# Six first weight loads instead of five, a first up-projection unit in the same steps, and another hand-written order: sliding-window attention with a squared-ReLU MLP on one core

## The chip, the core and the metric

The kernel runs on one core of a Trainium2 chip. The time is that of one execution on the device, in microseconds. TensorE (PE) multiplies, VectorE (DVE) and ScalarE (ACT) do the elementwise work, GpSimd (POOL) issues the loads, which convert float32 to bfloat16 on their way, and SyncE (SP) issues transposes by DMA and the stores. Each engine works through its own instructions in the order in which they are written, and waits for others by semaphores.

## The reference

Eight heads of causal attention with a window of 128 keys and an ALiBi bias, then an MLP without biases whose activation is the square of ReLU:

```python
scores = scale * np.matmul(q, k.transpose(0, 1, 3, 2))        # B=8, H=8, S=576, D=64
mask = (rel >= 0) & (rel < window)                            # window = 128
scores = np.where(mask, scores + bias[None], -1000000000.0)
...
attn = attn / (np.sum(attn, axis=-1, keepdims=True) + 1e-09)
...
x = np.ascontiguousarray(attn_out.transpose(0, 2, 1, 3)).reshape(B * S, H * D)   # 4608 x 512
h = x @ w_in                                                  # w_in 512 x 2048
r = np.maximum(h, 0.0)
g = r * r
return (g @ w_out).astype(np.float32)                         # w_out 2048 x 512
```

## The kernel before

**Tiling.** The 4608 tokens are 40 blocks m: for each of the 8 batches four of 128 tokens and one of 64. The MLP goes over nine groups g of 512 tokens. Attention of later blocks and the MLP of earlier groups run mixed.

**The order.** Every piece of work is a task with a name, planned by `plan.add`; which engine does it, in which buffer or bank, and in which place is written out by hand in the string `ORDER` (lines 60 to 216, some 1,800 items). `Plan.order` (line 272) walks through it and emits the tasks one by one. An item is `name:engine:places`, with a, d, g and s for ACT, DVE, POOL and SP, none for PE. Within an engine the written order is the order of execution. `Plan.order` also estimates start times from constants (`LAND`, `D_ST`, `dma=`, `lat=`); the only thing that these decide in what is emitted is how many filler matmuls `fill` (line 423) puts into an estimated gap of PE in the first microseconds.

**Names.** These are the items that the prediction uses:

- `lk m`, `lq m`, `lkq m`, `lv m`: loads of a block's k, q, both, and v, issued by POOL (lines 608, 614 and 621). `w_in n`, `w_out n`: the loads of the weights (lines 545 and 548). `PIECES` gives the loads of `w_in` in 128-column groups.
- `tp m`, `ev m`: transposes of k and q by PE (line 677) and their copies out, for the first eight blocks; later blocks have `kqT m`, a transpose by DMA that SP issues (line 662). It waits for its `lkq m` and for all the weights, takes one of 7 `kqT` tiles and frees one of 4 `kq` tiles.
- `s m`: scores (line 734); `e m`: exponentials (line 768); `m m`: masks (line 756); `pv m.0`, `pv m.1`: probabilities times values, in two halves of the heads (line 844); `r`, `n`: the reciprocals of the sums and the normalisation (lines 860 and 873).
- `xp m`, or from block 8 on `x m`: the transpose of the attention output into `xT`, by PE (line 893) and by SP's DMA (line 880).
- `u g.r.e`: a step of the up-projection of groups 0 to 2 (line 993); `UNITS` gives the token ranges r and the steps e of each, in 128-column groups. `reluu`, `squ`: its ReLU and its square.
- `us`, `ut`: sums of weights and of x for the products `f g.u.p` (line 1087), the up-projection of groups 3 to 8 by Strassen's scheme, with u from 0 to 3 and products p from 1 to 7. `s1`, `s2`, `s5`: copies of a product out of PSUM into one of eight `f` tiles (lines 444 and 446, on DVE or ACT); `c11`, `c12`, `c22`: sums (line 1108); then ReLU and square.
- `S1` to `S4` (line 1395) and `p g.p.z` (line 1249): the down-projection, by the same scheme, with its own copies into the same eight `f` tiles and sums into them (lines 1330 and 1335), and `st g.p.t`, the stores of the result out of an `f` tile by SP (line 1288). The tile is free again when the store has landed.

**What holds a task up** is the engine's order, its data, the buffer that it takes (the last user must be done), and, for a DMA of POOL, the one eight before it.

Of the kernel before, what the change touches and what calls it, by code (L numbers as in the profile page):

```python
# [15 lines left out]
FIRST = ["k0", "k1", "i0", "v0", "v1", "k2", "v2", "k3", "v3", "i1", "o0", "i2", "i3", "i4", "o1", "o2", "o3", "k4", "k5", "v4", "k6", "k7", "v5", "v6", "v7"]  # L16
# [6 lines left out]
N_PE = 8  # L23
# [5 lines left out]
D_KQ, D_X, D_ST = 2050.0, 1050.0, 750.0  # L29
# [34 lines left out]
ev2.1.0:d ev0.0.0:d one0.2:d tp1.0::7 s2 s0 e0.0:a e2.0:a e2.1:a ev1.0.0:d e0.1:a lv0:g lv2:g lq3:g lv1:g  # L64
w_in1:g w_in0:g w_in2:g lv3:g w_in3:g lk4:g lq4:g b1::0,4 tp1.1::3 pv2.0::7 ev1.1.0:d r2.0:d pv0.0::1 pv0.1::5
s1 n2.0:d r0.1:d r0.0:d n0.0:d tp3.1::3 n0.1:d xp0.0::6 pv2.1::2 x0.0:d r2.1:d ev3.1.0:d mask1.1:a e1.0:a e1.1:a
table:a pv1.0::7 pv1.1::1 b3::5,0 n2.1:d u0.0.1::4 r1.0:d r1.1:d n1.0:d n1.1:d xp2.0::6 s3 u0.0.0::3 xp1.0::2
dist0:d x2.0:a e3.0:a x1.0:a mask1.7:a reluu0.0.0:a:0 u0.2.0::7 mask0.3:a mask1.2:a mask0.1:a mask1.6:a e3.1:a
u0.1.0::1 u0.1.1::6 pv3.0::5 pv3.1::2 u0.2.1::3 u0.0.2::0 squ0.0.0:d one1.2:d reluu0.1.0:a:1 mask0.2:a
reluu0.2.0:a:2 one1.8:d r3.0:d squ0.1.0:d one1.7:d r3.1:d n3.0:d n3.1:d xp3.0::1 x3.0:d one1.5:d reluu0.2.1:a:3  # L70
one1.6:d squ0.2.1:d squ0.2.0:d reluu0.1.1:a:0 mask1.5:a mask1.4:a mask0.7:a mask0.5:a mask1.3:a mask1.0:a
reluu0.0.2:a:1 u0.1.2::7 tp4.0::5 tp4.1::2 ev4.1.0:d squ0.0.2:d u0.2.2::3 ev4.0.0:a reluu0.0.1:a:3 s4.0::6,1
s4.1::0,5 reluu0.1.2:a:2 e4.0:a lk5:g reluu0.2.2:a:1 lk6:g lq5:g lv5:g lq6:g w_in4:g tp5.0::2 u0.0.3::4
u0.3.0::7 tp5.1::6 squ0.0.1:d one1.1:d one1.0:d squ0.1.2:d ev5.0.0:d e4.1:a mask0.0:a mask0.4:a mask0.6:a m4.0:d
ev5.1.0:d squ0.1.1:d lk7:g lv4:g lv6:g lq7:g w_out3:g w_out0:g lv7:g w_out2:g w_out1:g e4.3:a reluu0.3.0:a:3
# [12 lines left out]
zerov10:d s1_0:d:0 kqT10:s ws1.0:d zerokqT11:d kqT11:s squ1.1.1:d p0.2.1 u1.1.5::7 u1.1.0::0 reluu1.1.0:a:3
reluu1.0.5:a:0 reluu1.1.5:a:1 u1.1.7::1 squ1.1.0:d ws1.2:d reluu1.1.7:a:2 u1.1.2::5 u1.1.6::3 squ1.1.7:a
reluu1.1.2:a:3 reluu1.1.6:a:2 u1.1.3::0 lkq12:g lv12:g lkq13:g lkq14:g s8.0::4,7 s8.1::1,5 ws0.2:d c11_0:d  # L90
S4.0.1:d S4.0.0:d squ1.1.5:d e8.0:a e8.1:a e8.2:a e8.3:a p0.5.0::6 u1.1.4::3 s9.0::4,7 s9.1::1,5 p0.5.1 kqT12:s
m8.0:d ws1.1:d m8.1:d reluu1.1.4:a:1 e9.0:a e9.1:a pv8.1::3 pv8.0::4 p0.6.0 p0.6.1 squ1.1.4:d S1.1.0:d
reluu1.1.3:a:1 e9.2:a s5_0:a:1 e9.3:a p0.3.0 lv10:g lv13:g lkq15:g m9.0:d r8.0:d n8.0:d squ1.0.5:d pv9.0::7
zerov11:d m9.1:d r8.1:d us0.1:d S3.0.1:d pv9.1::0 p0.3.1 lv11:g r9.1:d n8.1:d s10.0::1,4 s10.1::5,3 ws1.3:d
squ1.1.6:a s2_0:a:2 c12_0:d us3.1:d r9.0:d n9.0:d n9.1:d ws0.3:d e10.0:a e10.2:a e10.3:a m10.1:d us2.1:d e10.1:a
squ1.1.2:a x8:s p0.7.0 p1.2.0::6 p1.2.1 s12.0::1,5 s12.1::7,3 p0.7.1 lkq16:g e12.0:a e12.3:a squ1.1.3:a e12.2:a
e12.1:a x9:s m10.0:d S2.1.0:d us1.1:d pv10.0::0 pv10.1::4 pv11.0::1 c22_0:d r11.0:d p1.1.0::3 p1.1.1 p0.4.0
r10.0:d S1.1.1:d m12.1:d m12.0:d n11.0:d r10.1:d s1_1:a:3 c11_1:d S2.1.1:d pv11.1::7 pv12.0::5 pv12.1::1 p0.4.1
p1.6.0 r12.1:d n10.0:d r12.0:d n12.0:d S3.1.1:d n10.1:d S3.1.0:d S4.1.1:d r11.1:d n11.1:d u2.0.7::6
reluu2.0.7:a:0 s3_0:a:4 u2.0.6::0 u2.0.3::5 reluu2.0.6:a:2 reluu2.0.3:a:3 squ2.0.3:d n12.1:d us0.3:d squ2.0.6:d  # L100
u2.0.5::4 reluu2.0.5:a:1 kqT13:s kqT14:s kqT15:s kqT16:s lkq17:g lv15:g lkq18:g lv14:g s13.1::6,2 s13.0::7,0
e13.0:a e13.2:a e13.3:a x11:s x12:s p1.5.0::5 p1.5.1 s14.0::1,4 s14.1::7,6 x10:s u2.0.4::2 p1.6.1 S4.1.0:d
e13.1:a m13.0:d m13.1:d s5_1:a:5 e14.0:a e14.1:a s2_1:a:6 e14.3:a squ2.0.5:d p1.3.0 e14.2:a pv13.1::0 pv13.0::1
r13.0:d r13.1:d n13.0:d n13.1:d p1.3.1 m14.1:d s15.0::4,6 s15.1::7,1 u2.0.1::0 p1.7.0 e15.0:a e15.3:a e15.2:a
e15.1:a lkq19:g lv16:g lkq20:g lv17:g c12_1:d us3.3:d us1.3:d squ2.0.7:d st0.7.2:s kqT17:s st0.2.0:s x13:s
kqT18:s st0.7.3:s kqT19:s kqT20:s s16.0::4,5 s16.1::1,7 u2.0.2::6 p1.7.1 us2.3:d m14.0:d e16.0:a e16.1:a
reluu2.0.4:a:3 m16.0:d c22_1:d reluu2.0.1:a:2 squ2.0.1:a e16.3:a e16.2:a u2.1.3::4 u2.1.7::5 reluu2.1.7:a:1
m15.0:d m16.1:d squ2.1.7:d u2.1.1::2 pv14.0::0 pv16.0::7 pv14.1::1 pv16.1::5 reluu2.1.3:a:0 squ2.0.4:d
reluu2.0.2:a:2 squ2.0.2:a reluu2.1.1:a:1 r16.0:d n16.0:d r14.1:d r14.0:d n14.0:d r16.1:d m15.1:d n16.1:d p1.4.0
# [134 lines left out]
class Plan:  # L244
# [5 lines left out]
    FIRST = {"POOL": 1100.0, "SP": 1150.0, "ACT": 1150.0}  # L250
    LAND = {"POOL": 2400.0, "SP": 2200.0, "ACT": 900.0}
# [81 lines left out]
def kernel(  # L333
# [65 lines left out]
    L = N_LEAD  # L399
# [84 lines left out]
    for part in (1, 0):  # L484
        key = EARLY + 2 if part else -1e5 + 1100
# [972 lines left out]
```

## Time and profile before

| | |
|---|---|
| time, median of 3 runs | 294.30 us (293.76 to 294.39) |
| the profiled execution | 293.62 us, of which the span is 291.9 us |
| PE busy | 281.3 us (96%) |
| VectorE busy | 250.7 us (86%) |
| ScalarE busy | 218.9 us (75%) |
| POOL busy | 106.4 us (36%) |
| DMA | 39.64 MB, mean 136 GB/s |

The span runs from the first to the last instruction. Busy time is that of an engine's instructions; an engine that waits is idle. In a row of a timeline the first number is the start in us from the start of the span, the second how long the group lasted, then the engine, the line of the kernel, the operation, the output tile, the input tiles and the count. Brackets at its end give the idle time ahead of it and what ended that. In a row of the waits stand the engine, its line, what it waited for, and the total, the count and the longest wait. Landing times of DMAs are counted from their issue. SPq is SP's instruction queue, in which its transposes and stores are issued; DMA stands for the transfer itself.

### The profile page before, as it was taken

Reading aid. Unit: us, or ns where it says so; the run is one execution under the profiler, and the core shown is the slowest. Engines: PE = TensorE matmul, PEld = TensorE weight load, DVE = VectorE, ACT = ScalarE, POOL = GpSimd, SP = SyncE. Lnnn points to the kernel's source line nnn. Section 1 sums busy time; section 2 is a strip of 40 time slices with the busy share of each in tenths; the row PEclk is TensorE's granted clock in tenths of the full one; section 3 lists DMA queues with packets and bytes.
Section 4 is the critical chain, followed back from the end, with each engine's and each line's share of the span. In section 5 each row is a group of like instructions: output and inputs, shape, how many; then the busy total and the mean of one; then the engine's idle time right before and its main releaser. Section 6 shows DMA issues by size and latency. Waiting matters only on the chain.

```text
span 291.9 us, 8707 instructions
## 1 busy us (share of the span) xinstructions
PE 281.3 (96%) x3480; PEld 243.6 (83%) x3480; DVE 250.7 (86%) x610; ACT 218.9 (75%) x431; POOL 106.4 (36%) x132
## 2 busy tenths in 40 slices
PE   6899999998999999999999999989999999999994
PEld 2688999886888988888888889868898888888884
DVE  2556888897868899999999999979999998999864
ACT  4679976875378786799989998888786846976800
POOL 8968643582663922441737363051000000000000
PEclk9999999999999999999999999999999999999999
DMA  9999999999999999999999999999641222010054
GB/s 125 167 194 172 183 200 155 141 141 159 170 161 175 173 169 168 149 160 177 172 167 142 174 164 140 145 156 150 180 93 57 56 66 63 20 36 2 0 159 151
DMA packets 171497, 39.64 MB, mean 136 GB/s; under 512 B 156992, under 2 KB 171456, under 8 KB 171456
## 3 DMA queue, kind: packets, MB, share of 16 engines
q0 software_dynamic: 115184, 18.10, 92.1%
q1 hardware_dynamic: 55520, 20.39, 41.0%
q10 hardware_dynamic: 752, 0.59, 0.7%
q8 instruction: 27, 0.44, 0.6%
q14 instruction: 14, 0.11, 0.1%
HBM read 36.70 MB, written 9.44 MB: 158 GB/s over the span
## 4 chain that ended last, share of the span: by engine, by line
PE 75%; DMA 11%; POOL 7%; DVE 2%; issue 2%; ACT 1%; SPq 1%; POOLq 0%; DVEq 0%
PE o L1249 31%; PE h L1087 23%; PE h L993 10%; PE pv L844 5%; PE s L734 4%; DMA kq<-in_q_dram 3%; DMA out_dram<-f 3%; DMA vt<-in_v_dram 2%; POOL kq L608 2%; DMA kqT<-kq 2%; POOL kq L614 2%; SPq L880 1%; POOL vf L621 1%; POOL w_in_sb L545 1%; ACT rt L960 1%
## 5 line engine op out<-in xcount | busy, mean ns | idle before, releaser
L1249 PEld LDWEIGHTS <-g 128*128 128x128 bf16 x704 | 67.7, 98 | 8.1
L768 ACT ACTIVATE P<-s 128x512 bf16<-128x512 f32 x120 | 65.0, 622 | 6.0 <-PE s L734 5.8
L614 POOL DMA_DIRECT2D kq<-in_k_dram x32 | 27.2, 851 | 82.3 <-DMA kqT<-kq 77.8
L1249 PE MATMUL o<-w_out_sb,g 128*128 128x256 bf16 x432 | 54.0, 273 | 0.0
L960 ACT ACTIVATE rt<-h 128x512 bf16<-128x512 f32 (+1 forms) x73 | 42.4, 602 | 14.9 <-PE h L993 11.0
L1108 DVE TENSOR_TENSOR rt<-h,f 128x512 bf16<-128x512 f32 x72 | 48.2, 680 | 1.3 <-ACT rt L960 0.6
L993 PE MATMUL h<-xT,w_in_sb 128*128 128x128 bf16 (+1 forms) x512 | 46.6, 246 | 0.1
L952 ACT ACTIVATE g<-rt 128x512 bf16<-128x512 bf16 x70 | 43.3, 642 | 3.6 <-DVE rt L1113 3.0
L446 ACT ACTIVATE f<-h 128x512 f32<-128x512 f32 x63 | 36.3, 605 | 11.9 <-PE h L1087 9.9
L993 PEld LDWEIGHTS <-w_in_sb 128*128 128x128 bf16 x512 | 39.1, 98 | 4.2 <-DMA w_in_sb<-in_moe_w_in_dram 0.3
L1087 PE MATMUL h<-xT,w_in_sb 128*128 128x256 bf16 x288 | 41.7, 273 | 0.0
L1087 PEld LDWEIGHTS <-w_in_sb 128*128 128x128 bf16 x384 | 36.0, 98 | 5.5 <-issue 0.5
L1249 PE MATMUL o<-wsum,sums 128*128 128x256 bf16 x288 | 35.7, 273 | 0.0
L756 DVE TENSOR_TENSOR P<-P,masks 128x1024 bf16<-128x1024 bf16 x48 | 32.2, 681 | 3.5 <-ACT P L768 2.7
L1249 PE MATMUL o<-wsum,g 128*128 128x256 bf16 x272 | 34.8, 273 | 0.0
L954 DVE TENSOR_TENSOR g<-rt 128x512 bf16<-128x512 bf16 (+1 forms) x75 | 29.9, 413 | 5.0 <-ACT rt L960 4.6
L873 DVE TENSOR_TENSOR x<-pv,rec 128x256 bf16<-128x256 f32 (+1 forms) x80 | 31.6, 413 | 0.6
L621 POOL DMA_DIRECT2D vt<-in_v_dram x36 | 30.9, 876 | 3.3 <-DMA w_in_sb<-in_moe_w_in_dram 1.7
L1087 PEld LDWEIGHTS <-us 128*128 128x128 bf16 x288 | 27.8, 98 | 4.7 <-issue 1.2
L1249 PEld LDWEIGHTS <-sums 128*128 128x128 bf16 x288 | 27.6, 98 | 3.6
L614 POOL DMA_DIRECT2D kq<-in_q_dram x32 | 27.5, 861 | 1.9 <-PE xp L893 1.4
L446 ACT ACTIVATE f<-o 128x512 f32<-128x512 f32 x30 | 18.3, 609 | 13.1 <-PE o L1249 12.0
(81 smaller groups left out, 389.4 us busy)
## 6 DMA issues: line engine op xcount, KB each, us to landing
out_dram<-f SPq DMA_DIRECT2D x62, 128.0 KB, 2.2
kq<-in_k_dram POOLq DMA_DIRECT2D x31, 128.0 KB, 7.8
kq<-in_q_dram POOLq DMA_DIRECT2D x31, 128.0 KB, 8.2
vt<-in_v_dram POOLq DMA_DIRECT2D x28, 128.0 KB, 7.9
w_out_sb<-in_moe_w_out_dram POOLq DMA_DIRECT2D x4, 512.0 KB, 11.6
w_in_sb<-in_moe_w_in_dram POOLq DMA_DIRECT2D x3, 512.0 KB, 8.4
out_dram<-f SPq DMA_DIRECT2D x13, 64.0 KB, 2.1
vf<-in_v_dram POOLq DMA_DIRECT2D x4, 128.0 KB, 5.1
```

Of the source, the lines that this page charges most:

```text
L446: nc.scalar.activation(o, i, AF.Copy)
L614: nc.gpsimd.dma_start(view(kq[s_kq[m].idx], i), source(src, m, split))
L621: nc.gpsimd.dma_start(tile_of(s_v[m])[0:n, :, 0:D], source(v, m))
L756: nc.vector.tensor_tensor(flat(Pt[sP.idx], w), flat(Pt[sP.idx], w), flat(masks, w), op=ALU.mult)
L768: nc.scalar.activation(flat(Pt[sP.idx], slice(2 * i, 2 * i + 2)), sS[i].tile.rearrange("p (j t) -> p j t", j=2)[:, :, lo:hi], AF.Exp, bias ...
L873: nc.vector.tensor_tensor(o, heads(sv)[0:n, :, 0:D], sr.tile[0:n, :].unsqueeze(2).to_broadcast([n, 4, D]), op=ALU.mult)
L952: nc.scalar.activation(o, i, AF.Square, bias=0.0, scale=1.0)
L960: nc.scalar.activation(rts[srt.idx][:, 0:n], slot.tile[:, 0:n], AF.Relu, bias=0.0, scale=1.0)
L993: nc.tensor.matmul(slot.tile[:, f * w:(f + 1) * w], w_in_sb[:, cc, fc * 128:(fc + 1) * 128], xT[:, cc, lo % (XR * 128):lo % (XR * 128) + w ...
L1087: nc.tensor.matmul(slot.tile[:, j * 256:j * 256 + 256], a, b_, start=fresh and j == 0 and c == 0, stop=c == 1, skip_group_check=True)
L1108: nc.vector.tensor_tensor(rts[srt.idx], slot.tile, other(), op=ALU.add)
L1249: nc.tensor.matmul(slot.tile[:, z * 256:z * 256 + 256], stationary(c), moving(c), start=fresh and z == 0 and c == 0, stop=c == F - 1, skip ...
```

## The change

Three things change: the sizes of the loads of `w_in`, the steps of the first unit `u0.0`, and `ORDER`.

```diff
-FIRST = [..., "k3", "v3", "i1", "o0", "i2", "i3", "i4", "o1", ...]
+FIRST = [..., "k3", "v3", "i1", "o0", "i2", "i3", "i4", "i5", "o1", ...]
-D_KQ, D_X, D_ST = 2050.0, 1050.0, 750.0
+D_KQ, D_X, D_ST = 2050.0, 1050.0, 760.0
-UNITS = {0: [(0, 128, [2, 2, 4, 4, 4]), (128, 128, [4, 4, 4, 4]), ...
+UNITS = {0: [(0, 128, [1, 1, 2, 4, 4, 4]), (128, 128, [4, 4, 4, 4]), ...
-PIECES = [2, 2, 4, 4, 4]
+PIECES = [1, 1, 2, 4, 4, 4]
-    LAND = {"POOL": 2400.0, "SP": 2200.0, "ACT": 900.0}
+    LAND = {"POOL": 2400.0, "SP": 2500.0, "ACT": 900.0}
-        ns = 870.0 * n / 128
+        ns = (870.0 if m < N_PE else 870.0) * n / 128
+        land = None if m < N_PE else 2400.0
```

`land` is handed as `lat` to the tasks `lkq` and `lv`. It has the value that they had from `LAND`. It and the other constants are numbers of the estimate alone; with them the filler matmuls at the start go from 16 to 12.

`ORDER` is written anew. Most tasks keep their neighbourhood; banks and tiles are assigned anew. The items of POOL, from the first loads of v on, with the moved ones in both:

```diff
-lv0 lv2 lq3 lv1 w_in1 w_in0 w_in2 lv3 w_in3 lk4 lq4 lk5 lk6 lq5 lv5 lq6 w_in4 lk7 lv4 lv6 lq7 w_out3 w_out0 lv7 w_out2 w_out1
+lv0 lv1 lv2 lq3 w_in2 w_in0 w_in1 w_in3 lv3 w_in4 lk4 lq4 lk5 lq5 lk6 lq6 w_in5 lv4 lv5 lk7 lv6 lq7 lv7 lkq9 w_out2 w_out0 w_out3 w_out1
-lkq9 lkq8 lkq10 lv9 lkq11 lv8 lkq12 lv12 lkq13 lkq14 lv10 lv13 lkq15 lv11 lkq16
+lkq8 lkq10 lv9 lkq11 lv8 lkq12 lv12 lkq13 lkq14 lv10 lv13 lv11 lkq15 lkq16
```

Pieces of SP's order around the blocks 21 and 35, and one earlier (other items of SP between them are left out where the dots stand):

```diff
-kqT8 kqT10 kqT11 kqT12 x8 x9 ... kqT20 ... st0.2.1
+kqT8 kqT10 kqT11 st0.2.1 kqT12 x8 x9 ...
-... kqT22 kqT23 x17 st1.3.0 ... x19 st1.3.1 x18 x20 kqT24 x21 st1.4.3 kqT25
+... kqT22 st0.4.2 kqT23 st1.3.1 st1.3.0 x19 x18 x20 kqT24 x17 x21 kqT25
-... kqT34 x30 x29 x28 st3.7.2 kqT35
+... x28 ... kqT34 kqT35 st3.7.2 x30 x29
```

PE does the same work but for the fillers, in nearly the same order. Some of its items moved: `u0.0` now has the steps `u0.0.2 u0.0.0 u0.0.1` (of 2, 1 and 1 column groups) where `u0.0.1 u0.0.0` (2 and 2) stood; `pv11.0` stands ahead of `pv10.0`; `pv15.1` behind `s17` and not ahead of it; `p2.5.0` behind `f3.0.2`, `f3.0.1` and `f3.0.5`, not ahead of them. Between ACT and DVE some tasks change sides: twelve squares of 512 columns go from DVE to ACT, four copies of `xp` from ACT to DVE. In all DVE has five instructions fewer and ACT ten more. Two stores of the last group, `st8.7.2` and `st8.7.3`, are issued by ACT, not by SP; POOL has one load more.

More of the change, by code (lines that the diff above doesn't have):

```diff
@@ L93 @@
[L93 to L102, printed above, removed]
@@ new lines @@
+r30.0:d m32.1:d r31.0:d n30.0:d n31.0:d r30.1:d n31.1:d pv32.1::7 pv32.0::3 s2_4:a:0 sqc22.5.0:a reluc11.5.1:a
+p4.7.0 p4.7.1 sqc11.5.1:a c12.5.1:d:1 c22.5.1:d:0 r32.0:d sqf5.0.4:d r32.1:d n32.0:d n30.1:d f5.1.4
+reluc12.5.1:a s5_4:a:5 sqc12.5.1:a reluf5.1.4:a:3 reluc22.5.1:d sqc22.5.1:d n32.1:d f5.2.1::4 f5.2.2::2
+s1.5.2:a:3 sqc12.5.0:d S1.5.0:d c11.5.2:d:1 c22_4:d s33.1::3,1 s33.0::0,7 f5.2.6 p4.3.0 p4.3.1 f5.2.5::2 e33.0:a
+e33.1:a e33.3:a s2.5.2:a:4 e33.2:a m33.0:d kqT34:s kqT35:s st3.7.2:s x30:s x29:s f5.2.7 pv33.0::0 s5.5.2:a:3
```

299 lines of the change are left out of this document (152 added, 147 removed).

## The prediction

> **What bounds the kernel now.** The page comes first: the span, and the busy times of the engines.
>
> ```profile
> span 291.9 us, 8707 instructions
> PE 281.3 (96%) x3480; PEld 243.6 (83%) x3480; DVE 250.7 (86%) x610; ACT 218.9 (75%) x431; POOL 106.4 (36%) x132
> ```
>
> TensorE (PE) works for 281.3 of 291.9 us. An order that does the same matmuls can therefore gain at most the 10.6 us in which PE is idle, and most of that is out of reach. The second view, what PE waited for, names the waits. The third, the busy times by stretch, says where the other engines are as full as PE (the first number of a row is its length, then PE, PEld, DVE, ACT and POOL).
>
> ```profile
> PE wm L645 <- DVE sums L464: 2.5, 1, 2.5
> PE pv L844 <- DMA vt<-in_v_dram: 1.4, 1, 1.4
> PE h L1087 <- DVE f L444: 1.0, 1, 1.0
> PE tp L677 <- DMA kq<-in_q_dram: 0.4, 1, 0.4
> ```
>
> ```profile
> 2.50:26.00 23.50, 22.03 (x299) 16.37 (x300) 10.79 (x46) 16.53 (x44) 20.21 (x24) 1.00 1.89 177
> 72.00:120.00 48.00, 48.00 (x622) 41.74 (x619) 40.59 (x101) 32.91 (x63) 23.39 (x28) 1.00 1.81 165
> 120.00:180.00 60.00, 59.96 (x773) 51.93 (x768) 59.32 (x142) 57.51 (x113) 28.74 (x34) 1.00 1.93 164
> 193.00:287.70 94.70, 94.61 (x999) 83.61 (x997) 87.79 (x192) 63.83 (x119) 4.98 (x7) 1.00 0.38 79
> 287.70:291.90 4.20, 0.26 (x5) 0.08 (x2) 0.42 (x2) 0.00 (x0) 0.00 (x0) 0.95 0.43 127
> ```
>
> The change leaves 2.5 us of idle time at the start (PE waits for a VectorE memset) and some 3.9 us at the end (4.20 less 0.26, the last copies and stores) as they are. What an order can move is 1.5 us at the start (23.50 less 22.03), the wait of 1.4 us for a v tile, and the wait of 1.0 us for a copy on VectorE. From 120 to 180 us VectorE is busy for 59.32 of 60 us beside PE's 59.96, so PE has no slack there against a late VectorE.
>
> **The change part by part.** All durations below are from the profiled execution, 293.62 us long (its span is 291.9); the median of the timed runs is 294.30, 0.68 more.
>
> *Six loads for five, and the first unit in steps of the same sizes.* The same bytes of w_in go in one load more; u0.0 has one step more for the same matmuls. These rows are the POOL timeline, the DMA issues (last number: us to landing), the weight loads of PE, the chain of waits and PE's timeline, in that order.
>
> ```profile
> 9.29 2.32 POOL L545 DMA_DIRECT2D w_in_sb<-in_moe_w_in_dram  x3
> w_in_sb<-in_moe_w_in_dram POOLq DMA_DIRECT2D x1, 256.0 KB, 5.5
> w_in_sb<-in_moe_w_in_dram POOLq DMA_DIRECT2D x1, 512.0 KB, 8.3
> w_in_sb<-in_moe_w_in_dram POOLq DMA_DIRECT2D x1, 256.0 KB, 6.1
> 19.07 0.90 PEld L993 LDWEIGHTS <-w_in_sb 128*128 128x128 bf16 x16 [0.27 <-DMA w_in_sb<-in_moe_w_in_dram]
> 13.99 10.03 DMA kq<-in_q_dram
> 24.06 0.40 PE tp L677 x4
> ```
>
> The three issues take 2.32 us, 0.77 each, so they start at 9.29, 10.06 and 10.83 and land at 14.79, 16.16 and 19.13. The third, columns 4 to 7, is what PE waits 0.27 us for at 19.07. In the new order the same bytes stand ahead of it (w_in2 of two groups, then w_in0 and w_in1 of one each, then w_in3). Where 256 KB went as one load, now 128 KB go twice. By the 512 KB load, 128 KB cost (19.13 − 16.16)/4 = 0.74 us, and by the 256 KB one 1.37/2 = 0.69. The other bound is an issue of 0.77 for each. So the two cost 1.38 to 1.54 where one cost 1.37: this piece lands 0.0 to 0.2 us later. The chain then goes through the load of q block 4, issued at 13.99 behind the same bytes, and landing at 24.02, which PE's transpose of it at 24.06 had to wait for. What the first unit gains or loses before 24 us by up to the length of that wait (0.4) ends there. Value: 0, with bounds of 0 and +0.2 (the piece's lateness, had the wait behind it no room).
>
> By the Trainium skill, "DMA: Bandwidth & Descriptors", section "Anatomy of one DMA — SWDGE (gpsimd) path", a load issued by GpSimd takes about 2.0 us plus its bytes over 436 GB/s. Taken as time that each load adds to a queue, that makes an estimate of 2 us for the extra one; the rows show the second 256 KB landing 1.37 us behind the first, so by them two loads overlap in whatever is fixed. By the page the sum would be about 295, by the rows it stays below.
>
> *The v tile of block 11 (lv11).* Its row in the waits is PE's 1.4; the chain of waits and the timeline of that stretch show why.
>
> ```profile
> 60.74 0.88 POOL vt L621 x2
> 62.23 1.73 POOL kq L614 x2
> 63.95 7.21 DMA vt<-in_v_dram
> 69.08 0.73 PE L844 MATMUL pv<-vt,P 128*64 128x65 bf16 x17
> 71.21 0.38 PE L844 MATMUL pv<-vt,P 128*64 128x65 bf16 x7 [1.40 <-DMA vt<-in_v_dram]
> ```
>
> POOL issued lkq15 (1.73 us for its two loads) and only then lv11, which landed at 71.16. The new order has lv10, lv13, lv11, lkq15. So lv11 leaves 1.73 us earlier and would land at 69.43, and PE, which was through with pv10 at 69.08 + 0.73 = 69.81, finds it there. Worth −1.40 at best; if the landing gains only half of what the issue gained, −0.87. I take −1.3: the order around pv11 is also changed (pv11.0 now ahead of pv10.0), which can cost a tenth. What is late next here is lkq15, later by one v issue (at most the 0.88 of the row of two); its transpose kqT15 stands behind kqT13 and kqT14 on SP, which cover that.
>
> *The store st3.7.2.* VectorE's copy s1.5.3 needs a free f tile; the tile's last user was this store.
>
> ```profile
> 176.44 2.01 SPq L662 DMA_TRANSPOSE kqT<-kq  x1
> 181.09 1.34 SPq L880
> 182.48 1.28 SPq L880
> 183.80 8.08 DMA out_dram<-f
> 192.00 0.69 DVE L444 COPY f<-h 128x512 f32<-128x512 f32 x1 [1.62 <-DMA out_dram<-f]
> 192.74 0.49 PE L1087 MATMUL h<-ut,us 128*128 128x256 bf16 x3 [1.04 <-DVE f L444]
> ```
>
> On SP the store stood behind kqT34 (176.44 to 178.45) and x30, x29 and x28, and left at 183.80. Now it stands behind kqT34 and kqT35, ahead of x30 and x29, so it leaves at about 180 instead of 183.8, and with its 8.08 us lands near 188. The copy, which VectorE was free for at 190.4 (1.62 before 192.00), no longer waits: −1.04. The other end is 0: kqT35 is a transpose of the same kind, and if it waits for its k and q, the store waits in SP's queue behind it. I take −1.04. What is late next is x30, behind kqT35 and the store (2.0 + 0.6 us), whose readers are the f6 steps, behind all of f5.
>
> *Transposes that do not come earlier with PE.* Against these gains stand SP's transposes of x, whose landing PE meets with little to spare. The rows are SP's timeline, the landing of the transpose (DMA issues), PE's timeline; twice; then all transposes of x.
>
> ```profile
> 97.81 3.99 SPq L880 DMA_TRANSPOSE xT<-x  x3
> xT<-x SPq DMA_TRANSPOSE x1, 8.1
> 108.63 1.04 PE L1249 MATMUL o<-wsum,sums 128*128 128x256 bf16 x8
> 109.50 1.04 PE L1087 MATMUL h<-xT,w_in_sb 128*128 128x256 bf16 x8
> 128.49 2.30 SPq L880 DMA_TRANSPOSE xT<-x  x1
> xT<-x SPq DMA_TRANSPOSE x1, 7.4
> 136.66 0.61 PE L1087 MATMUL h<-xT,w_in_sb 128*128 128x256 bf16 x4
> DMA to landing us min/median/max: 2.3/6.0/8.9
> ```
>
> The third of the first rows, x15, leaves at 100.5 (97.81 and two thirds of 3.99) and lands at 108.6. PE's f3.0.2 of group 3 began at 109.50, 0.9 us later. In the new order p2.5.0 (the eight matmuls from 108.63 to 109.50, 0.87 us) has gone from ahead of f3.0.2 to behind it, and PE arrives 1.3 us earlier, so f3.0.2 would stand at 107.3. If x15 lands where it did, PE waits 1.3 us there and lv11's gain is given back. If x15 leaves as much earlier as PE is, little is given back. But pv15.1, the PE step that its input needs, has been put behind the scores s17, so it cannot gain the whole. In group 4 x21 leaves at 128.49 and lands at 135.9, 0.77 us ahead of f4.0.1 at 136.66: if it stays, 0.5 of a gain of 1.3 is given back there (1.3 − 0.77). Value +0.9, the middle of these two (1.3 and 0.5); the bounds are 0, where both move with PE, and 1.3.
>
> *The rest of the order.* PE's other work is the same but for four filler matmuls fewer at the start, where PE waits anyway. Twelve squares go from VectorE to ScalarE and four copies of xT the other way; in the one stretch where both are full, 120 to 180 us, their shares stay as they are, and ScalarE has room elsewhere (32.91 of 48.00 us before, 63.83 of 94.70 after). Two of the last stores go from SP's queue to ScalarE's: 0, behind the same last copies. Every one of 1,798 places is new, and the order before left one wait of 1.4 us and one of 1.0. I charge +0.4 for new waits of the kind, between 0 and 1.4 (one as long as the longest of the old).
>
> The sum: 293.62 − 1.3 − 1.04 + 0.9 + 0.4 = 292.58, and 0.68 more on the scale of the median: **293.2 us**. With nothing given back and no new wait it is 294.30 − 1.40 − 1.04 = 291.9; with lv11 at −0.87, or with all 1.3 given back, it is 293.7.
>
> **The rivals.**
>
> *All is given back.* x15 stays at 108.6, the gain of the store is 0 because kqT35 waits, or VectorE, at 59.32 of 60 us, does not let PE run ahead: 294.30 − 1.3 + 1.3 = 294.3. For it speaks the saturated stretch: a gain ahead of 120 us must pass through 60 us in which VectorE has 0.7 to spare. Against it, the second wait lies behind that stretch and is taken away where it stands.
>
> *Slower: x21 behind x17.* SP's x17 has moved from behind kqT23 to just ahead of x21. One mechanism: x17 takes 1.2 us of SP's queue (97.81's three took 3.99) at the place where x21 has 0.77 to spare, and two transposes share the transfer. With the longest landing that a transpose of x shows, 8.9, x21 lands at 128.49 + 1.2 + 8.9 = 138.6. f4.0.1, and with it PE, would stand 1.9 us behind its old 136.66, whatever was gained before it. Less the 1.04 of the store that is +0.9, so 295.2. From a landing of x21 at 137.7 the store's gain is gone; from 138.3 on the kernel is slower by what can be measured (0.6). For it speaks that SP is issuing without a pause there; against it, that the median landing is 6.0, by which it would be down at 135.7.
>
> *The sixth load sets the pace.* If the extra load takes a place of its own in the queue, an issue (0.77) and the turn of a 256 KB load (1.37) although it adds no bytes, then lq4 lands 2.1 us later, and PE's transpose of it, which had no room, moves with it: 293.2 + 2.1 = 295.3. Against it stands that the 1.37 between two landings is what 256 KB take by the larger load too (2.97/2 = 1.49), which leaves nothing for a fixed part. The rule on GpSimd's loads in the Trainium skill, read as above, would have this case.
>
> *It does not do what it says.* The first unit starts earlier, by its first 128 columns, but ends no earlier, as lq4 holds PE at 24.06: part of my forecast.
>
> **How the numbers follow.** A measurement of this kernel can tell about 0.2% (0.6 us) from no change, so faster means below 293.7 and slower above 294.9. The likeliest case (293.2, its own range 291.9 to 293.7) has 0.55; all given back (294.3) 0.17; slower by x21 or another late transfer (295.2, or more where two come together) 0.23; the sixth load 0.05. Faster: 0.54, nearly all of the first. Same: 0.18, the second and the first's upper edge. Slower: 0.28, the last two. The range goes from 291.8 to 295.5, which holds the slower case's own time.
>
> **What would show it.** Right: among PE's waits the rows for vt (1.4) and for f L444 (1.0) are gone; the wait for lq4 near 24.06 is still there; the store in question leaves near 180 and lands near 188; the tail is still 4.2 us. For the giving back: a new wait of PE on xT near 107 to 109 or near 136, of 0.3 to 1.3 us. For the slower case: PE waits over 1 us for xT near 137. Wrong altogether: PE past 24.06 at a time that differs by over 0.5 us, or PE busy less than 281 us with waits on VectorE or ScalarE between 120 and 180 us, which would mean that the moved squares set the pace.

## The result, and the profile after

The changed kernel takes 293.82 us in the median of 20 runs and the kernel before 293.30 us in runs beside it; the ratio is 1.0042, with a 95% interval of 1.0022 to 1.0063. It is slower by 0.4%, some 1.2 us. The ratio leaves out executions that ran slow, so it lies above the quotient of the two medians (1.0018). Run 7 below, the changed kernel but for one load, gives 1.0047 on another chip. The predicted 293.2 us is close to the number, but the prediction said faster, and the change made the kernel slower. That the number came close is luck: it was built on 294.30 us for the kernel before, which took 293.30 beside the changed one. As ratios, 0.996 was forecast and 1.0042 measured.

The page of the profiled execution, its two rows that answer to those of before:

```profile
span 292.7 us, 8720 instructions
PE 281.6 (96%) x3476; PEld 243.2 (83%) x3476; DVE 248.8 (85%) x605; ACT 223.4 (76%) x439; POOL 107.2 (37%) x133
```

The span is 0.8 us longer, PE's work 0.3. So it is again a question of where PE waits. The waits of PE after the change, without the 2.5 us at the very start, which are as before (engine, line, what it waited for, the total, the count, the longest; lines have moved down by one):

```profile
PE h L1088 <- DVE ut L1057: 1.8, 1, 1.8
PE s L735 <- DMA kqT<-kq: 0.9, 1, 0.9
PE pv L845 <- DMA vf<-in_v_dram: 0.9, 1, 0.9
PE pv L845 <- DMA vt<-in_v_dram: 0.5, 1, 0.5
PE tp L678 <- DMA kq<-in_q_dram: 0.4, 1, 0.4
```

The two waits that the prediction wanted gone have shrunk: vt from 1.4 to 0.5, and the copy on VectorE from 1.0 to nothing. In their place stand two that were not there: 1.8 us for `ut`, which VectorE makes from transposed x, and 0.9 for a `kqT`. The wait for `vf` is 0.5 longer (0.4 before). Busy times by stretch, first those rows of before that were not shown, then those of after (the stretch, its length, busy time of PE, PEld, DVE, ACT and POOL):

```profile
26.00:69.00 43.00, 43.00 (x632) 38.48 (x630) 37.77 (x93) 35.67 (x73) 24.34 (x31) 1.00 1.78 166
69.00:72.00 3.00, 1.60 (x31) 1.34 (x30) 1.48 (x6) 1.56 (x4) 0.34 (x1) 1.00 1.77 153
180.00:190.00 10.00, 9.89 (x118) 8.51 (x115) 9.98 (x26) 8.18 (x16) 2.66 (x3) 1.00 2.23 143
190.00:193.00 3.00, 1.96 (x29) 1.48 (x28) 1.38 (x3) 2.17 (x5) 0.00 (x0) 1.00 1.18 217
```

```profile
2.50:26.00 23.50, 21.54 (x292) 15.83 (x292) 10.60 (x39) 15.99 (x42) 20.64 (x25) 1.00 1.90 176
26.00:69.00 43.00, 42.01 (x617) 37.64 (x612) 37.39 (x99) 34.49 (x70) 24.72 (x31) 1.00 2.05 165
69.00:72.00 3.00, 2.52 (x43) 2.00 (x43) 2.63 (x6) 2.42 (x6) 1.14 (x2) 1.00 1.17 68
72.00:120.00 48.00, 46.06 (x592) 39.49 (x591) 39.06 (x96) 30.77 (x59) 21.63 (x26) 1.00 1.85 165
120.00:180.00 60.00, 60.00 (x766) 51.65 (x765) 59.41 (x146) 56.39 (x110) 29.88 (x36) 1.00 1.92 170
180.00:190.00 10.00, 10.00 (x127) 8.84 (x125) 9.78 (x28) 8.84 (x17) 1.18 (x2) 1.00 1.90 144
190.00:193.00 3.00, 3.00 (x36) 2.53 (x36) 3.00 (x7) 2.76 (x6) 1.63 (x2) 1.00 0.90 219
287.70:292.70 5.00, 1.74 (x24) 1.49 (x22) 1.66 (x4) 0.00 (x0) 0.00 (x0) 0.88 0.50 153
```

Length less PE's busy time is PE's idle time, and the differences add up to the result:

| stretch, us | idle before | idle after | difference |
|---|---|---|---|
| 2.5 to 26 | 1.47 | 1.96 | +0.49 |
| 26 to 69 (s8 waits for kqT8) | 0.00 | 0.99 | +0.99 |
| 69 to 72 (pv11) | 1.40 | 0.48 | −0.92 |
| 72 to 120 (f3.0.5 waits for x15) | 0.00 | 1.94 | +1.94 |
| 180 to 193 (s1.5.3) | 1.15 | 0.00 | −1.15 |
| the end, from 287.7 | 3.94 | 3.26 | −0.68 |

That is +0.67. The stretches left out give −0.1, and PE's longer work +0.3; the sum is the 0.8 us of the spans. The two gains that I had forecast, 2.1 us in sum, were outweighed by 2.9 us at two places, both of which stand on transposes that SP issues.

**The first place: kqT8.** The last load of the weights, w_out1, among the DMA issues of before, and of after (count, KB, us to landing; it is issued at 32.04 and at 33.88):

```profile
w_out_sb<-in_moe_w_out_dram POOLq DMA_DIRECT2D x1, 512.0 KB, 13.3
```

```profile
w_out_sb<-in_moe_w_out_dram POOLq DMA_DIRECT2D x1, 512.0 KB, 15.9
kqT<-kq SPq DMA_TRANSPOSE x1, 12.2
```

The second row of after is kqT9. SP's timeline, the chain of waits and PE's timeline of after show when it left, and what came of it (the four transposes of the first row are kqT9 at 37.16 and, from 51.53 on, kqT8, kqT10 and kqT11):

```profile
37.16 18.63 SPq L663 DMA_TRANSPOSE kqT<-kq  x4
```

```profile
35.86 15.61 DMA kq<-in_q_dram
```

```profile
58.01 0.23 PE L735 MATMUL s<-kqT,kqT 64*128 64x128 bf16 x2 [0.94 <-DMA kqT<-kq]
```

In the changed order lkq9 is loaded ahead of the four w_out loads. It lands early, so its transpose kqT9 goes out at 37.16, 10 us sooner than before, and needs 12.2 us. In the chain of waits of before it is this row:

```profile
47.55 6.12 DMA kqT<-kq
```

For as long as kqT9 runs, the loads of the weights run against it, and w_out1 lands at 49.8 where it landed at 45.3. (A part of these 4.5 us are the bytes of lkq9, which now stand ahead of w_out1; run 12 tells the two apart.) The load of lkq8, behind them, takes 15.61 us and lands at 51.47 (48.93 before); kqT8, issued then, lands at 57.96 (54.40 before), when PE has been waiting for 0.94.

**The same lateness at pv11.** The chain of waits of after between 52 and 72 us (start, length, what):

```profile
52.86 8.37 DMA kqT<-kq
...
61.76 1.72 POOL kq L615 x2
...
63.48 1.54 POOL vt L622 x2
65.03 6.15 DMA vt<-in_v_dram
...
71.22 0.63 PE pv L845 x15
```

lv11 now stands ahead of lkq15, but it was issued at 65.03 where it used to be at 63.95, because POOL stood in front of lkq14 until the transpose kqT10 had landed at 61.23 and freed a kq tile. It landed at 71.18; before it was 71.17. PE waits less for it only because PE is itself a microsecond late by then.

**The second place: x15.** SP's timeline, the chain and PE's timeline of after:

```profile
100.23 3.99 SPq L881 DMA_TRANSPOSE xT<-x  x3
```

```profile
102.88 9.20 DMA xT<-x
```

```profile
112.69 0.61 PE L1088 MATMUL h<-ut,us 128*128 128x256 bf16 x4 [1.84 <-DVE ut L1057]
```

x15 left at 102.88 and landed at 112.09; before it left at 100.5 and landed at 108.6. It is the last of the three transposes in both, and all three left 2.4 us later. PE had run through f3.0.2 and f3.0.1 and stood 1.84 us before f3.0.5, with p2.5.0, which it could have done, behind f3.0.5 in its order.

### The profile page after: what moved, and what is told of

It reads as the page before. It is cut to its first block, busy times and chain, and to the rows that moved or that the text cites. A ratio compares the mean times of both kernels' runs of the same rounds, so it can differ in the third digit from the quotient of the medians.

```text
span 292.7 us, 8720 instructions
## 1 busy us (share of the span) xinstructions
PE 281.6 (96%) x3476; PEld 243.2 (83%) x3476; DVE 248.8 (85%) x605; ACT 223.4 (76%) x439; POOL 107.2 (37%) x133
## 4 chain that ended last, share of the span: by engine, by line
PE 73%; DMA 17%; POOL 6%; SPq 1%; issue 1%; DVE 0%; ACT 0%; POOLq 0%; DVEq 0%
PE o L1250 31%; PE h L1088 25%; DMA kq<-in_q_dram 9%; PE h L994 6%; PE pv L845 5%; PE s L735 4%; DMA xT<-x 3%; DMA kqT<-kq 3%; POOL kq L609 2%; DMA vt<-in_v_dram 2%; POOL w_in_sb L545 1%; POOL vf L622 1%; POOL kq L615 1%; PE o L1352 1%; SPq L881 1%
## 5 line engine op out<-in xcount | busy, mean ns | idle before, releaser
L953 ACT ACTIVATE g<-rt 128x512 bf16<-128x512 bf16 x82 | 50.1, 634 | 2.1 <-DVE rt L1114 1.3
L446 ACT ACTIVATE f<-h 128x512 f32<-128x512 f32 x64 | 37.0, 600 | 10.8 <-PE h L1088 10.2
L1250 PE MATMUL o<-wsum,sums 128*128 128x256 bf16 x288 | 36.4, 273 | 0.0
L1088 PE MATMUL h<-ut,us 128*128 128x256 bf16 x192 | 27.5, 273 | 1.8 <-DVE ut L1057 1.8
L955 DVE TENSOR_TENSOR g<-rt 128x512 bf16<-128x512 bf16 (+2 forms) x64 | 25.2, 407 | 3.9 <-ACT rt L961 2.9
```

Source lines behind the costliest of these rows:

```text
L446: nc.scalar.activation(o, i, AF.Copy)
L953: nc.scalar.activation(o, i, AF.Square, bias=0.0, scale=1.0)
L1088: nc.tensor.matmul(slot.tile[:, j * 256:j * 256 + 256], a, b_, start=fresh and j == 0 and c == 0, stop=c == 1, skip_group_check=True)
L1250: nc.tensor.matmul(slot.tile[:, z * 256:z * 256 + 256], stationary(c), moving(c), start=fresh and z == 0 and c == 0, stop=c == F - 1, skip ...
```

## The experiments

Every ratio is that to the kernel before, run beside it on the same chip, with its 95% interval; for the changed kernel it is 1.0042. The difference of two such ratios carries 0.3 to 0.4%, 1 us or more, so the times alone tell only the larger effects apart, and the traces have to say which wait went. A trace is one execution: PE's wait for `vt`, 1.40 in the profile before, is 0.84 in that of run 4, where nothing ahead of it was changed. A wait counts as removed here when several traces agree. In the profiles of the first four runs the lines are 8 lower, since their order is written in fewer lines.

**1. lkq9 behind the weights, in the changed kernel** (a_lkq9).

```diff
-lv7:g lkq9:g w_out2:g w_out0:g w_out3:g w_out1:g
+lv7:g w_out2:g w_out0:g w_out3:g w_out1:g lkq9:g
```

> The changed kernel with one load moved: lkq9 goes behind the four w_out loads again, as in the kernel before. Theory: in the changed kernel lkq9 lands at 37.07 us, its transpose kqT9 is issued at 37.16 and runs against the weights, w_out1 lands at 49.80 instead of 45.32, lkq8 at 51.47 instead of 48.93, kqT8 at 57.96 instead of 54.40, and PE waits 0.9 us for it. With the load back: w_out1 lands before 47, kqT8 before 56, PE's wait for kqT is gone, and lv11 lands before 70, so that pv11's wait of 0.5 us goes too. Time 1.0 to 1.5 us below the changed kernel, if nothing behind takes it. Rival: the queue is full either way; PE comes earlier to f3.0.5, which waits for x15 whatever PE gained, the wait of 1.8 us there grows by what was won, and the time stays within 0.3 us.

292.32 us, ratio 1.0007 (0.9982 to 1.0033), 1.0 us below the changed kernel. SP's timeline, and the longest of PE's waits behind the start:

```profile
47.83 6.57 SPq L655 DMA_TRANSPOSE kqT<-kq  x4
```

```profile
PE h L1080 <- DVE ut L1049: 2.0, 1, 2.0
```

The transposes start at 47.83, w_out1 lands at 45.51, kqT8 at 54.91 and lv11 at 68.55. The rows for kqT and for vt are gone from the waits, and so they are in runs 5 and 6, which make the same move. Run 7, with lkq9 still ahead, waits 1.5 us for kqT, and lv11 lands at 70.49 there. So both belonged to this one move. The rival, that all of it would be given back at f3.0.5, falls: that wait grew by 0.2 only, since x15 came earlier with PE.

**2. The chain to x15, in the changed kernel** (a_x15).

```diff
-S1.2.1:d S3.2.1:d ... r15.0:d r15.1:d n15.0:d n15.1:d ... x16:s x14:s x15:s ... f3.0.2::3 f3.0.1::7 ... f3.0.5::4 p2.5.0::5
+r15.0:d r15.1:d n15.0:d n15.1:d S1.2.1:d S3.2.1:d ... x14:s x16:s x15:s ... p2.5.0::5 f3.0.2::3 f3.0.1::7 ... f3.0.5::4
```

> The changed kernel with three moves around the transpose x15: r15 and n15 (four instructions) go ahead of the sums S1.2.1 and S3.2.1 on VectorE, x14 goes ahead of x16 on SP, and p2.5.0 goes back ahead of f3.0.2 on PE. Theory: the changed kernel's x15 left at 102.88 and landed at 112.09 because its input stood behind pv15.1 (put behind s17) and behind two sums, and PE stood 1.8 us at f3.0.5 (ut3.0 on VectorE) for it. With the moves x15 leaves at about 101.6 and lands near 111, p2.5.0 fills 0.87 us of the wait, and the rest is below 0.3 us. Time 1.5 to 2.0 us below the changed kernel. Rival: the landing of x15 is set by the transfers in the queue and not by its issue, so it stays at 112; then only the 0.87 us of p2.5.0 are won, and a wait of about 0.9 us stays at f3.0.5.

292.82 us, ratio 1.0021 (0.9995 to 1.0047): 0.6 us below the changed kernel, which the intervals cannot tell from nothing, where 1.5 to 2.0 were expected. It is nearer to what the rival gives. Only the time of this run is used; runs 5 and 6 take the moves apart.

**3. lv11 alone, in the kernel before** (b_lv11).

```diff
-lv10:g lv13:g lkq15:g ... zerov11:d ... lv11:g
+lv10:g zerov11:d lv13:g lv11:g lkq15:g ...
```

> The kernel before with lv11 ahead of lkq15 (and the zero fill of its tile right behind lv10), nothing else. My prediction's term: lv11 leaves 1.73 us earlier, lands at 69.4, PE's wait of 1.40 us at pv11 goes, and the time falls by 0.9 to 1.4 us, less what the next transposes give back (x15 has 0.9 us to spare at f3.0.2, x21 0.77 us). Rival: lv11 lands as late as it did in both profiles (71.17 and 71.18), because its landing follows the queue and not its issue; the time stays within 0.3 us. Second rival: the wait goes, and x15 and x21 take the whole of it: new waits for xT at f3.0 or f4.0 of about 1 us in sum, time within 0.3 us.

291.79 us, ratio 0.9981 (0.9954 to 1.0008). The issue of lv11 went from 63.95 to 62.11, its landing from 71.17 to 67.85, and the wait for vt is gone; the longest that are left behind the start:

```profile
PE tp L669 <- DMA kq<-in_k_dram: 1.2, 1, 1.2
PE h L1079 <- DVE f L436: 0.7, 1, 0.7
```

The first of these rows stands at 9.55 us, at a load that the edit does not touch; it is anything up to 1.2 in the profiles of this order, and PE begins the transpose of q block 4 at 24.08 all the same (24.06 before). No wait for xT has come up in its place, at x15 or at x21. The wait for vt is gone in runs 8 and 11 too, which make the same move. By itself, then, the move does what my term for it said (0.8 to 1.4 us by the traces without it), and nothing was given back; the timed gain of 0.2% is smaller than the 1.4 us of the trace, and its interval holds both.

**4. st3.7.2 alone, in the kernel before** (b_st372).

```diff
-kqT34:s x30:s x29:s x28:s st3.7.2:s kqT35:s
+kqT34:s kqT35:s st3.7.2:s x30:s x29:s x28:s
```

> The kernel before with kqT35 and then st3.7.2 ahead of x30, x29 and x28 on SP, nothing else. My prediction's term: the store leaves near 180 in place of 183.80 us, lands near 188, VectorE's copy s1.5.3 no longer waits, PE's wait of 1.04 us at f5.3.6 goes, time 1.0 us below the kernel before. Rival: x28, x29 or x30 land late for f6.0, or VectorE, busy 59.32 of 60 us just before, is what PE waits for anyway: the wait moves to another VectorE result within 5 us, and the time stays within 0.3 us.

292.31 us, ratio 0.9999 (0.9966 to 1.0032): no gain that can be measured. SP's timeline, the chain, and PE's wait:

```profile
176.36 5.58 SPq L654 DMA_TRANSPOSE kqT<-kq  x2
181.99 0.61 SPq L1280 DMA_DIRECT2D out_dram<-f  x1
```

```profile
181.99 8.37 DMA out_dram<-f
```

```profile
PE h L1079 <- DVE f L436: 0.3, 1, 0.3
```

The two transposes kqT34 and kqT35 held SP for 5.58 us together, of which the first took 1.2 (176.36 to 177.59). The second, right behind it, took over 4 us of SP's time. The store was moved past three transposes of x, which had cost 3.9 us, and behind one of kq, which cost more, and left at 181.99 in place of 183.80; it landed at 190.36 in place of 191.88. VectorE still waited for it. PE's wait is 0.3 in place of 1.0, but by that alone the step is not shown to gain: in runs 3 and 8, where the store stands as before, the wait is 0.7 and nothing.

**5. lkq9 behind the weights, and p2.5.0 ahead of f3.0.2** (a_lkq9_p25): the edit of run 1 and the last move of run 2.

> The changed kernel with lkq9 behind the w_out loads (as in the run with that move alone) and p2.5.0 ahead of f3.0.2 again on PE. Theory: x15's landing is set by work that does not depend on where p2.5.0 stands, so its 0.87 us fill that much of the wait of some 2.0 us before f3.0.5, which becomes 1.1 to 1.2; time 0.9 us below the run with lkq9 alone. Rival: the wait is passed on, since the next step on VectorE is late too; time within 0.3 us of that run.

292.16 us, ratio 0.9997 (0.9969 to 1.0025), 0.3 us below run 1, which the intervals cannot tell from 0.9. The waits say more:

```profile
PE h L1088 <- DMA xT<-x: 0.6, 1, 0.6
PE pv L845 <- DVE rt L1109: 0.4, 1, 0.4
...
PE h L1088 <- DVE ut L1057: 0.2, 1, 0.2
```

x15 landed at 109.83 (109.95 in run 1), and of the wait of 2.0 us are left 0.6 and 0.2. But a new wait for VectorE of 0.4 stands at 115.6 us (and in run 6 at 115.0), so the rival has a part in it: some is passed on, and what is won in sum is 0.8, about the 0.87 of p2.5.0.

**6. The whole chain to x15 as well** (a_fix): run 5, the moves of run 2, and `pv15.1` ahead of `s17`.

```diff
-s17.0::0,2 s17.1::6,5 pv15.1::3
+pv15.1::0 s17.0::3,2 s17.1::6,5
```

> The same, and the chain to x15 brought forward: pv15.1 ahead of s17 on PE, r15 and n15 ahead of S1.2.1 and S3.2.1 on VectorE, x14 ahead of x16 on SP. Theory: x15 leaves 1.2 us earlier than in the run with lkq9 alone (101.11 us there), its landing moves with it (109.95 there, so to about 108.8), and together with p2.5.0 the wait before f3.0.5 falls from some 2.0 to below 0.3 us; time about 1.8 us below the run with lkq9 alone, below the kernel before. Rival: the transfers in the queue set the landing, x15 leaves earlier and lands at 109.9 all the same; then only the 0.9 us of p2.5.0 are won.

291.54 us, ratio 0.9981 (0.9956 to 1.0006), 1.8 us below the changed kernel. x15's input was there 1.7 us sooner, at 98.73 us, but SP sent x15 out only at 100.46 (101.11 in run 1), behind x14 and x16. It landed at 109.16, and a wait of 0.50 us stays:

```profile
109.76 0.96 PE L1088 MATMUL h<-ut,us 128*128 128x256 bf16 x7 [0.50 <-DVE ut L1057]
```

So the two theories of run 2 share it: SP's queue passes on 0.65 of the 1.7 us that the input gains, and p2.5.0 does most of the rest. The ratio is that of run 3: with both causes taken out, the change gives about what the move of lv11 gives alone.

**7. Five loads for six, in the changed kernel** (a_five): `PIECES` and the unit as before the change, w_in0 and w_in1 as one load, their two steps as one.

```diff
-w_in2:g w_in0:g w_in1:g w_in3:g lv3:g w_in4:g ... w_in5:g
+w_in1:g w_in0:g w_in2:g lv3:g w_in3:g ... w_in4:g
```

> The changed kernel with five w_in loads (2, 2, 4, 4, 4 groups) and the first unit in the steps 2, 2, 4, 4, 4, in the new order: the two loads of one group go as one, and their two steps as one. My prediction's term: neutral; w_in's columns 4 to 7 land 0 to 0.2 us earlier, PE's transpose of q block 4 starts within 0.2 us of where it does with six loads (24.35), the time is within 0.3 us of the changed kernel. Rival by the fixed cost of a load: the columns 4 to 7 and lq4 land 0.7 to 2 us earlier and the time falls by as much.

293.59 us, ratio 1.0047 (1.0016 to 1.0079), the same as the changed kernel. Columns 4 to 7 landed at 18.94 (19.17 in the changed kernel), q block 4 at 24.04 (24.30), and PE's transpose of it began at 24.09 in place of 24.35. These 0.2 to 0.3 us are no more than the profiles with six loads differ among themselves: there the columns landed at 18.79 (run 6) to 19.17, and the transpose began at 23.96 to 24.35. So no cost of the sixth load can be seen, and no loss hangs on it. By the fixed 2.0 us of the Trainium skill ("DMA: Bandwidth & Descriptors", section "Anatomy of one DMA — SWDGE (gpsimd) path"), read as a time that loads in a row add up, it would have been an estimated 2 us; the measurement decides, and as a time from issue to landing the page's figure isn't touched by it.

**8. lv11, and two of the last stores by ScalarE, in the kernel before** (b_lv11_tail): run 3, and `st8.7.2:a`, `st8.7.3:a` for `:s`.

> The kernel before with lv11 ahead of lkq15, as in the run with that alone, and the stores st8.7.2 and st8.7.3 issued by ScalarE as in the changed kernel. In the profiles 3.6 us pass from the last VectorE copy to the end of the span before the change and 2.9 after it (3.3 with lv11 alone). Theory: the two stores on SP hold up the last two there, and on ScalarE they do not; the end comes 0.4 to 0.7 us sooner after the last copy, 2.9 to 3.0 us. Rival: the difference is that of single landings; it stays at 3.3 to 3.6 us, and the time is that of lv11 alone.

292.18 us, ratio 0.9992 (0.9954 to 1.0030), no different from run 3. The span of 288.3 us ends 3.5 us after the last copy (284.49 and 0.29): the shorter end of the changed kernel doesn't come from these two stores. Most of it lies behind the landing of the last store: from there to the end of the span it is 1.60 us in the profile before and 1.15 in that of the changed kernel, 1.5 to 1.6 in every run with the old order and 1.15 to 1.17 in every run with the new one. What makes it so was not tried.

This profile shows one thing more. The store `st3.7.2` stands where it stood before and left at 181.92, but it landed at 187.21, and VectorE did not wait for it:

```profile
188.30 0.68 DVE L444 COPY f<-h 128x512 f32<-128x512 f32 x1
```

**9 and 10. lkq9 ahead of the weights, in the kernel before, alone** (b_lkq9) **and with lv11 ahead of lkq15** (b_lkq9_lv11).

```diff
-lq7:g w_out3:g w_out0:g lv7:g w_out2:g w_out1:g ... lkq9:g lkq8:g
+lq7:g lkq9:g w_out3:g w_out0:g lv7:g w_out2:g w_out1:g ... lkq8:g
```

> The kernel before with lkq9 ahead of the four w_out loads, nothing else: the move that I hold to blame in the changed kernel, made in the kernel before. Theory: kqT9 is issued near 37 us in place of 47.55 and its transfer runs against the weights; w_out1 lands 3 to 4 us later than 45.3, lkq8 2 to 3 us later than 48.9, kqT8 near 58 in place of 54.4, PE waits 1.0 to 2.5 us for it at s8; the loads behind stay late, so that the wait for lv11 (1.4 us) stays too. Time 0.8 to 1.5 us above the kernel before. Rival: lateness at s8 is taken up by the 1.4 us of waiting at pv11 (lv11 lands where it did, 71.2), and the time stays within 0.4 us.

> The kernel before with both moves on POOL that the changed kernel makes: lkq9 ahead of the w_out loads, lv11 ahead of lkq15. Theory: lv11 alone won (0.9981 of the kernel before) because it landed at 67.85 instead of 71.17; with lkq9 ahead the slots of the k and q tiles come free later, the loads ahead of lv11 are issued later and it lands at 70 or later, while PE comes 1.0 to 2.5 us later by the wait at s8. So no wait at pv11, but a wait at s8 of about its size: the time is within 0.4 us of the kernel before. Rival: the two moves add up, and the time is that of lkq9 alone less 1.4 us.

298.06 us, ratio 1.0201 (1.0162 to 1.0240), and 298.33 us, ratio 1.0210 (1.0170 to 1.0250). It is slower, by some 6 us where 0.8 to 1.5 were expected, and at another place than I thought. PE's timeline, and busy times by stretch (the number behind POOL's is PE's granted clock), of run 9:

```profile
48.56 0.21 PE L844 MATMUL pv<-vt,P 128*128 128x65 bf16 x1 [4.61 <-DMA vt<-in_v_dram]
```

```profile
46.00:48.00 2.00, 0.00 (x0) 0.00 (x0) 0.00 (x0) 0.82 (x2) 0.00 (x0) 1.00 1.05 72
48.00:50.00 2.00, 1.44 (x19) 1.24 (x19) 0.42 (x3) 0.00 (x0) 0.68 (x1) 0.57 1.85 177
50.00:52.00 2.00, 2.00 (x12) 1.45 (x11) 1.97 (x6) 0.00 (x0) 0.68 (x1) 0.58 1.82 158
52.00:54.00 2.00, 2.00 (x23) 1.81 (x22) 2.00 (x5) 1.09 (x2) 0.41 (x1) 1.00 1.33 94
```

In this order lv7 stands among the weights, and with kqT9 running against it (from 36.06 to 48.56) it landed at 48.52; before it was 40.26. PE stood 4.61 us for it. The changed kernel escapes this, because it has lv7 ahead of lkq9. With PE so late, lv11 is in time wherever it stands (it landed at 73.40, PE came at 75.9), and the move of lv11 wins nothing: the two are not additive.

**11. lv11, and the store much earlier, in the kernel before** (b_best): run 3, and `st3.7.2` right behind `st3.7.3`.

```diff
-st3.7.3:s st3.3.0:s x26:s st3.3.1:s kqT33:s x27:s ... kqT34:s x30:s x29:s x28:s st3.7.2:s kqT35:s
+st3.7.3:s st3.7.2:s st3.3.0:s x26:s st3.3.1:s kqT33:s x27:s ... kqT34:s x30:s x29:s x28:s kqT35:s
```

> The kernel before with lv11 ahead of lkq15 and st3.7.2 right behind st3.7.3 on SP, ahead of kqT33, kqT34 and the three x. Theory: its data are there since 155 us, it leaves near 164 and lands near 171, and the f tile is free long before the copy s1.5.3 at 190; PE's waits for vt (1.4) and for f on VectorE (1.0 in the profile before) are both gone, and nothing takes their place. Time 1.5 to 2.0 us below the kernel before and 0.5 to 1.0 below lv11 alone. Rival: the copy waits for another f tile or VectorE is late by its own work (59.32 of 60 us busy from 120 to 180), so the second wait moves and the time is that of lv11 alone.

291.06 us, ratio 0.9971 (0.9946 to 0.9995), faster than both kernels. The store left at 162.97 and landed at 168.52, and VectorE goes straight on to the copy:

```profile
187.89 0.68 DVE L1108 TENSOR_TENSOR rt<-h,f 128x512 bf16<-128x512 f32 x1
188.49 0.68 DVE L444 COPY f<-h 128x512 f32<-128x512 f32 x1
```

Beside run 3 the time is 0.1% less, which the intervals cannot tell from nothing. The wait is gone, but in run 8 it is gone without this move, so what the move is worth is not shown.

**12. The load early, its transpose late, in the changed kernel** (a_kqT9).

```diff
-kqT9:s ... kqT8:s ... kqT10:s
+kqT8:s kqT9:s ... kqT10:s
```

> The changed kernel with kqT9 behind kqT8 on SP; the load lkq9 stays ahead of the w_out loads. It tells the load's place from the transpose's start. kqT8 waits for lkq8, so kqT9 can no longer start at 37 us. Theory: it is the transpose that holds up the weights, not the 256 KB of lkq9 ahead of them. Without it w_out1 lands near 47.2 (45.5 as with lkq9 behind, and 1.7 for its bytes) and not at 49.80, lkq8 near 49, kqT8 before 56, and PE's wait of 0.9 us at s8 is gone; the time is that of the run with lkq9 moved, 1.0 us below the changed kernel. Rival: the order of the loads does it; w_out1 stays near 49.8, kqT8 near 58, and the wait stays.

293.41 us, ratio 1.0038 (1.0006 to 1.0070). The mechanism is as the theory has it and the time is not. With kqT9 at 50.82 instead of 37.16, w_out1 landed at 47.55 (49.80 in the changed kernel), lkq8 at 49.28, kqT8 at 53.82, and the wait at s8 is gone. So of the 4.3 us by which w_out1 was later than in run 1 (45.51), the place of the load made 2.04 and the transpose 2.25. lkq8, which kqT8 waits for, was held up by the transpose alone: it landed at 49.18 in run 1. But a kq tile now comes free later, lkq12 leaves at 55.70 (51.37), kqT12, issued at 61.27, takes 8.8 us (4.9) and lands at 70.08, and s12 stands (SP's timeline, then PE's):

```profile
49.36 5.98 SPq L663 DMA_TRANSPOSE kqT<-kq  x4
61.27 1.25 SPq L663 DMA_TRANSPOSE kqT<-kq  x1
```

```profile
70.12 0.23 PE L735 MATMUL s<-kqT,kqf 64*128 64x128 bf16 x2 [2.32 <-DMA kqT<-kq]
```

## Why the prediction was wrong

**What was right.** That an order can only move PE's waits, and that the six loads and the new first steps are neutral (run 7). That PE meets the load of q block 4 after the first unit however that goes (24.35 with a wait of 0.44, 24.06 with one of 0.45 before): the 0.5 us more that PE stood for `vf`, since lv2 is one place back, end there, and the 0.3 us between the two starts are what profiles of one order differ by. That VectorE between 120 and 180 us would not set the pace (59.41 of 60 busy, PE 60.00). That x15 is where gains would be given back.

**The term for lv11 (−1.3).** Right for the move alone (run 3), wrong in this order. I took the issue to be 1.73 us earlier because the two loads of lkq15 no longer stand ahead of it. But POOL stood waiting for a tile, not working: in the profile before, too, it had waited 5.96 us for a transpose at lkq12. Which load stands ahead counts only as long as POOL runs through; and the move of lkq9, which I had in front of me in the order of POOL, made the transposes behind it, kqT8, kqT10 and kqT11, 3.6 to 6.2 us later. I listed lkq9 and gave it no price. That is the step that failed: I counted the loads as they stand in POOL's order, and not the transpose that the landing of a moved load lets go. This one move made the wait of 0.94 at s8, kept lv11's landing at 71.18, and is worth 1.0 us by run 1.

**The term for the transposes of x (+0.9, bounds 0 and 1.3).** This step failed too. The place was right, the reader and the size were not. f3.0.2 and f3.0.1 read the blocks 13 and 14 alone, and f3.0.2 began at 109.82, before x15 had landed; the first reader of x15 is the sum ut3.0, for f3.0.5. (f4.0.1, beside which I put x21, reads the blocks 17 to 19.) And I let x15 land at 108.6 at the latest, where it did before, and it landed at 112.09, for two reasons that the profile separates. It left 2.4 us later: its input was there at 102.68 and not at 99.37 (pv15.1 behind s17, then two sums ahead of r15 and n15 on VectorE), and x16 and x14, ahead of it in SP's queue, were late as well. And its landing took 9.2 us in place of 8.1. I had seen the first and used it only to say that x15 would not come earlier; the bound should have been open above. And I counted p2.5.0 as a change of PE's arrival where it was a loss of cover: in front of f3.0.2 its 0.87 us would have filled the wait (run 5).

**The term for the store (−1.04).** The wait is gone, but not by the step that I gave. The store left at 183.33 and landed at 191.06, where I had put it at about 180 and near 188: kqT35, ahead of it, held SP for 4.5 us (178.82 to 183.28) where I had counted 2.0. In run 4 it was 4.2. In the changed kernel PE and VectorE came to this place late enough to find the tile free. The wait of 1.0 us was slack for lateness ahead of it: of what was lost by 120 us, 1.15 came back here. Nor was it a fixed price: with the store unmoved it is 0.7 in run 3 and nothing in run 8. So what the step is worth stays open, in run 11 too, where the store really is early.

**The term for new waits (+0.4).** It stood for what I had not worked out, and was sized by the longest wait of the old order. The new wait at s8 alone came to 0.94.

**The rivals.** "Slower: x21 behind x17" did not happen: x21 landed at 136.08 and no wait for xT stands near it. The slower side came from the same kind of thing at x15 and kqT8, which stood in no line among the rivals. "All is given back" is nearest to what happened. The end of the kernel, which I took to be fixed, was 0.68 us shorter, 0.45 of it behind the last landing; why is open (run 8).

## What to carry to other kernels

A load that is moved forward also lets go what waits for its landing. Where that is a DMA, ask what it will run against; here a transpose that started 10 us sooner held up the weights, and everything behind them, through tiles that came free late. The place of an instruction in a queue says when it is issued only while the engine ahead of it is not waiting itself. And a wait that a change removes may have been room for lateness from ahead: look at what arrives there now, before it is booked as a gain.

## What the runs showed of the hardware

**A transpose by DMA holds up the loads beside it.** The DMA rate of the changed kernel between 37 and 49 us, in 40 slices of 0.3 us, and that of run 1, in which kqT9 starts at 47.83:

```profile
GB/s 212 205 208 205 242 191 205 198 201 205 201 212 205 198 201 200 195 187 192 198 201 198 197 192 194 192 201 195 201 196 241 169 177 146 25 18 13 162 177 158
```

```profile
GB/s 212 205 205 266 191 191 191 208 198 205 208 205 208 205 208 201 215 198 208 208 205 206 191 179 169 166 157 156 206 146 146 144 153 153 153 152 153 153 155 154
```

With the transpose in flight, three slices from 47.2 us on fall to 13 to 25 GB/s, and in run 9 there is such a hole as well (72 GB/s in the two microseconds from 46). Such a hole is no mark of the changed order: near 76 us, with two transposes in flight, the rate in the profile before falls to 0 to 10 GB/s for 1.2 us. What the early transpose costs the loads is the difference of run 12 to the changed kernel: without it w_out1 and lkq8 landed 2.2 us sooner. The transpose itself took 12.2 us, where kqT9 before took 6.1; all transposes of kq in the profile before took 2.9 to 11.1. What inside the DMA engines does it was not tried.

**Issuing a transpose takes SP 1.2 to 5.2 us** (the bounds for kq in the profile before). kqT35, right behind another of kq, held SP for over 4 us (run 4); behind a store it took 1.6 (before). Its inputs had landed at 173.33, before it was issued at 177.76, so it was not its data that it stood for. Nor does the neighbour alone decide: kqT10, right behind kqT8, took 1.2 in the profile before. The cause is open. A queue of SP is not priced by the count of what stands in it.

**A wait of 4.6 us costs more than itself.** In run 9 the granted clock was 0.57 and 0.58 in the two stretches after PE's idle time, and 1.00 again from 52 us. A step of 16 matmuls took 3.04 us there, and 1.91 ahead of the wait. The Trainium skill agrees ("TensorE: Matmul & The Clock Gate", section "What's actually happening"): after an idle window of some 3.4 us the clock is halved, until PE has been busy for about as long. The waits of up to 2.3 us (run 12) in the other runs left the clock at 1.00.
